# A first burst of eight query heads, output weights ahead of the fourth row tile, and the values transposed in two halves, in a fused attention and gated feed-forward kernel

## The chip, the cores and the metric

The kernel runs on one core of a Trainium2 chip. The core has five engines that work side by side, each on its own list of instructions: PE (TensorE, matrix products into the PSUM memory), ACT (ScalarE, functions of single elements), DVE (VectorE, element-wise work and reductions), POOL (GpSimd) and SP (SyncE, which here issues DMAs). An instruction that needs another engine's result waits for a semaphore, and all behind it on that engine waits too. The metric is the time of one execution on the device in microseconds, and of several runs the median.

## The reference

One layer: attention over a cached window of keys and values, times a gated feed-forward branch, plus the input. Cut to what is computed:

```
xn = layernorm(x)                                   # x: 2048 rows of 448
# attention: 16 query heads on 8 key/value heads of 256, the last 512 cached positions
q = (xn @ wq) in 16 heads
p = softmax(q @ k.T / 16)                           # no mask
s = concat(p @ v over the heads) @ wo
# gated feed-forward branch, 1792 wide
f = (gelu(xn @ w_gate) * (xn @ w_up)) @ w_down
out = x + s * silu(f)
```

All inputs and the output are bf16.

## The kernel before

The 2048 rows are four chunks (`NQC`) of 512 rows (`QC`), each of four tiles (`TPC`) of 128 rows. The kernel holds keys, values and weights in SBUF throughout. A recorder (`Rec`) collects the operations of each engine in the order in which the program calls them, and adds waits on semaphores where one operation needs what another writes, or writes what another still reads. So the order of the calls is the order on each engine. Three stages follow each other.

**Start (lines 301 to 441).** SP issues the loads in the order in which they are written: rows of tiles 0 and 1, the values of the last key/value head (`load_v7`), rows of tiles 2 and 3 (`load_x0`), the last head's rows of the output weights (`load_wo7`), then the feed-forward weights by slices. Two of the small weight loads go through ACT's queue. PE runs small matmuls on zeros (`warm`), then transposes the last head's values through the identity into one PSUM bank (`fold_tr`, L388), and ACT copies that bank to `vT` (`fold_copy`, L394). With `vT` and the loaded output weights PE makes `vw`, the product of the last head's values and their output weights (`fold`, L400, four products), so that the last head of each chunk goes straight from its probabilities to the output. Between these the first four tiles are normalised: statistics on DVE (L335, L336), standard deviation on ACT (L373), reciprocal and normalisation on DVE (L377, L339), transposes on PE (`ln_tr`, L357 and L359), and copies to `xnT` (`ln_copy`, L368 on DVE for tiles 2 and 3, L370 on ACT for tiles 0 and 1). On DVE the statistics of tiles 2 and 3 stand ahead of both their normalisations.

**Feed-forward (from `gate_up`).** For each chunk and each of 14 blocks `f` of the width, PE makes the gate and up products (L472), ACT applies gelu (L489) and DVE multiplies (L490). The row length of 448 is three and a half times 128, and so these products run as pairs of matmuls that use 64 rows of the array each, side by side (`two_blocks`). After each of the first three chunks PE makes the down products (`down`, L496). The last chunk's down products are kept for later: 4 tiles of 14 matmuls, which the table `fill` spreads over the first part of attention.

**Attention.** Head `i` counts from 0 to 63: sixteen heads for each of the four chunks. The queries of several heads are made at a time by a *burst* (`q_burst`, two_blocks again, 14 matmuls for each head), copied by ACT to the buffers `qT0` to `qT4` (L527), one for each pair of heads (`q_slot`). For each head and each row tile `t`, `scores(i, t)` makes one 128x512 product on PE (L552, two matmuls), the exponential with its row sum on ACT (L556), the reciprocal and scaling on DVE (L558, L559), and a DMA transpose of the probabilities `pr` to `pT`, issued by SP (`dmaT`, L252). The buffers `pr` are used in turn. Three heads behind, `values(i, e_)` multiplies `pT` by the values (L574), one half of the head's width at a time, and DVE copies the result to `oT`; it needs the transposes of all four tiles of its head. The output products (`outproj`, L604) follow later still, and DVE and POOL combine them with the feed-forward branch.

In this loop the order of the calls in one step is: `scores`; a share of `down` where `fill` has one; at even steps from the twelfth on, one `values`; at odd steps from head 7 on, a share of `outproj`; and the next burst of queries, if one is due. In the kernel before, the first burst is of four heads, ahead of the loop; the second, of four, comes after the step of head 3, tile 0; and then one of eight comes after tile 0 of heads 7, 15, 23 and so on.

Of the kernel before, what the change touches and what calls it, by code (L numbers as in the profile page):

```python
# [5 lines left out]
ACT = mybir.ActivationFunctionType  # L6
ALU = mybir.AluOpType
BF16 = mybir.dt.bfloat16
# [3 lines left out]
P = 128  # L12
# [132 lines left out]
def bass_recurrent_scan__sliding_block_cached__geglu_ffn__prompt_kernel(nc, A_x, A_k, A_v, A_wq, A_wo, B_x, B_wg, B_wu, B_wd, out):  # L145
    _, S, D = A_x.shape
    Hkv, Sk, Dh = A_k.shape[1], A_k.shape[2], A_k.shape[3]
    HD = A_wq.shape[1]
    Hq = HD // Dh
    W = min(4096, max(256, Sk // 4))  # L150
    F = B_wg.shape[1]
    QC, TPC, HP, KF = 512, 4, 64, 3
    NQC = S // QC
    NT = NQC * TPC
    NF, NJ, NE = F // P, W // P, Dh // P
# [6 lines left out]
    with es:  # L162
        off = [16512]

        def sb(name, shape, dt, at=None):
            n = 4 if dt == F32 else 2
            for x in shape[1:]:
                n *= x
            if at is None:
                at = off[0]  # L170
                off[0] += (n + 31) // 32 * 32
            return R.place(name, shape, dt, at), at + (n + 31) // 32 * 32

        ident, _ = sb("ident", [P, P], BF16)
# [11 lines left out]
        V, _ = sb("V", [P, NJ, Hkv, Dh], BF16)  # L186
# [20 lines left out]
        NPT, NQP = 4, 5  # L207
# [28 lines left out]
        def bank(b, n=512):  # L236
            return psum[:, b * 512:b * 512 + n]
# [5 lines left out]
        pe = lambda *a, **k: R.op("tensor", *a, **k)  # L243
        act = lambda *a, **k: R.op("scalar", *a, **k)
# [3 lines left out]
        def dma(eng, dst, src, w=(), r=(), after=(), lane=None):  # L248
            return R.op(eng, lambda e: e.dma_start(dst, src), r=r, w=w, dma=True, after=after, lane=lane)  # L249

        def dmaT(dst, src, w=(), r=(), after=(), lane=None):
# [9 lines left out]
             r=[("ident",)], w=[("ident",)])  # L261


        def load_x0(a, b):
            dma("sync", x4[:, a:b, :], x_view[:, 0, a:b, :], w=[("x4", t) for t in range(a, b)])
# [6 lines left out]
        def load_w(n, s):  # L272
            a, b = cuts[s] * P, cuts[s + 1] * P
            w, name, src, _ = w_gu[n]
            dma("sync", w[:, :, a:b], src[:, :, a:b], w=[(name, s)])

        def load_gu(s):
            load_w(0, s)
            load_w(1, s)
# [15 lines left out]
        def load_v7():  # L295
            dma("sync", V[:, :, Hkv - 1, :], v_view[:, :, Hkv - 1, :], w=[("V", "f")])

        def load_wo7():
            dma("sync", wo[:, NO - NE:NO, :], wo_v[:, NO - NE:NO, :], w=[("wo", "f")])
# [1 line left out]
        for t in range(2):  # L301
            load_x0(t, t + 1)
        load_v7()
        for t in range(2, TPC):
            load_x0(t, t + 1)
        load_wo7()
        load_gu(0)
        load_gu(1)
        load_gu6(5, NF, "sync")
# [71 lines left out]
        vT = actT[:, NF - 3:NF - 1, :]  # L381
        vT_keys = [("actT", NF - 3), ("actT", NF - 2)]

        def fold_tr():
            def run(e):
                for m in range(NE):
                    for j in range(NJ):
                        ins = e.transpose(bank(0).bitcast(BF16)[:, m * W + j * P:m * W + (j + 1) * P],  # L388
                                          V[:, j, Hkv - 1, m * P:(m + 1) * P], ident[:, :])
                return ins  # L390
            pe(run, r=[("V", "f"), ("ident",)], w=[("ps", 0)])

        def fold_copy():
            act(lambda e: e.activation(vT.rearrange("p m k -> p (m k)"), bank(0).bitcast(BF16), ACT.Copy),  # L394
                r=[("ps", 0)], w=vT_keys)

        def fold(j):
            def run(e):
# [12 lines left out]

        warm(32)
        fold_tr()
        for t in range(2):
            ln_stats(t)
# [48 lines left out]
        def two_blocks(ph, c, s, w, w6, keys, q0=0, q1=QC):  # L464


            def run(e):
                for k in range(KF + 1 - ph):
                    for lo in (0, HP):
                        m = (lo > 0) ^ ph  # L470
                        lhsT = w[m][lo:lo + HP, k, :] if k < KF else w6[lo:lo + HP, :]
                        ins = e.matmul(bank(s + m)[:, q0:q1], lhsT=lhsT, rhs=xnT[lo:lo + HP, c, k, q0:q1],  # L472
                                       start=ph == 0 and k == 0, stop=ph == 1 and k == KF - 1)
                return ins
            hard = [phase0[s]] if ph else []
            phase0[s] = pe(run, r=xn(c)[q0 // P:q1 // P] + keys, w=[("ps", s), ("ps", s + 1)], hard=hard)
# [30 lines left out]
        NI = NQC * Hq  # L507
        NG = NI // 4

        def q_slot(i):  # L510

            p = i // 2
            p = p if p < 3 else (p - 3) % NQP
            return qT[p], "qT%d" % p, i % 2

        def q_burst(i0, heads):

            c, h0 = divmod(i0, Hq)

            def part(n, ph):  # L520
                hp, e_ = divmod(n, 2)
                s, h = 2 * (n % 3 if heads == 8 else (0, 2, 1, 0)[n] if i0 else (n + 2) % 4), h0 + 2 * hp
                buf, name, _ = q_slot(i0 + 2 * hp)
                two_blocks(ph, c, s, [wq[:, :, h + m, e_ * P:(e_ + 1) * P] for m in range(2)],
                           wq6[:, h // 2, e_ * P:(e_ + 1) * P], wq_keys)
                if ph:
                    act(lambda e: e.activation(  # L527
                        buf[:, :, e_, :], psum[:, s * 512:(s + 2) * 512].rearrange("p (a q) -> p a q", a=2), ACT.Copy),
                        r=[("ps", s), ("ps", s + 1)], w=[(name, e_)])

            for n in range(heads + 1):
                if n < heads:
                    part(n, 0)
                if n:
                    part(n - 1, 1)
# [9 lines left out]
        def scores(i, t):  # L545
            g, n = (i % Hq) // 2, i * TPC + t
            b, s = 4 + n % 2, n % NPR
            buf, name, a = q_slot(i)

            def run(e):  # L550
                for k in range(NE):
                    ins = e.matmul(bank(b), lhsT=buf[:, a, k, t * P:(t + 1) * P], rhs=kT[:, g, k, :],  # L552
                                   start=k == 0, stop=k == NE - 1)
                return ins
            pe(run, r=[("kT", g), (name, 0), (name, 1)], w=[("ps", b)])
            act(lambda e: e.activation(pr[s][:, :], bank(b), ACT.Exp, scale=scale, accum_out=den[:, s:s + 1]),  # L556
                r=[("ps", b)], w=[("pr%d" % s,), ("den", s)])
            dve(lambda e: e.reciprocal(rden[:, s:s + 1], den[:, s:s + 1]), r=[("den", s)], w=[("rden", s)])  # L558
            dve(lambda e: e.tensor_scalar(pr[s][:, :], pr[s][:, :], rden[:, s:s + 1], None, op0=ALU.mult),  # L559
                r=[("pr%d" % s,), ("rden", s)], w=[("pr%d" % s,)])  # L560
            dst, key = p_slot(i)
            dmaT(dst[:, :, t * P:(t + 1) * P], pr[s][:, :], r=[("pr%d" % s,)], w=[(*key, t)], lane="p%d" % s)
# [22 lines left out]
        def n_pieces(G):  # L585
            return 3 * NE + NJ if folded(4 * G + 3) else 4 * NE
# [52 lines left out]
        def load_xr(c):  # L639
            dma("gpsimd", xr[:, :, :], x_view[:, c, :, :], w=[("xr", t) for t in range(TPC)])  # L640
# [11 lines left out]
        for c in range(NQC):  # L652
            lead = 6 if c == 0 else 2
            for f in range(NF + 1):
# [4 lines left out]
                t = (f - lead) // 2  # L659
# [13 lines left out]
                    load_piece()  # L673
        assert not pieces
        act(lambda e: e.activation(small[:, 2:3], small[:, 0:1], ACT.Exp), r=[("eps",)], w=[("warm",)])
        q_burst(0, 4)
        load_xr(0)

        fill = {}
        for d, slots in ((0, range(0, 4)), (1, range(4, 12)), (2, range(13, 17)), (3, range(17, 21))):  # L680
            for n, s in enumerate(slots):
                fill[s] = d, range(n * NF // len(slots), (n + 1) * NF // len(slots))
        pv = [(i, e_) for i in range(NI) if not folded(i) for e_ in range(NE)]
        outs = [(G, t) for G in range(NG) for t in range(TPC)]
        for i in range(NI):
            for t in range(TPC):
                scores(i, t)
                if 4 * i + t in fill:
                    down(NQC - 1, *fill[4 * i + t])

                early = i >= Hq and i % Hq == 2
                if t % 2 == 0 and early:
                    n = n_pieces(outs[1][0])
                    outproj(*outs[1], range(n * t // 4, n * (t + 2) // 4), b=6)
                elif t % 2 == 0 and 4 * i + t >= 12:
                    values(*pv.pop(0))
                if 7 <= i and t % 2 and not (i >= Hq and i % Hq == 6):
                    n = n_pieces(outs[0][0])
                    outproj(*outs[0], range(n * (t - 1) // 4, n * (t + 1) // 4))
                    if t == TPC - 1:  # L700
                        del outs[0:1 + early]
                if t == 0 and (i == 3 or i % 8 == 7) and i + 1 < NI:
                    q_burst(i + 1, 4 if i == 3 else 8)
            if i % Hq in (7, 9, 11, 13):
                silu(i // Hq * TPC + (i % Hq - 7) // 2)

# [40 lines left out]
```

## Time and profile before

| What | us |
|---|---|
| median of 3 runs | 558.26 (558.12 to 558.84) |
| the profiled execution | 558.57 |
| its span, first to last instruction | 556.8 |
| PE busy | 552.5 |
| ACT busy | 295.6 |
| DVE busy | 313.7 |
| first matmul of the feed-forward stage (L472) | at 10.39 |
| first matmul of the scores (L552) | at 133.56 |

The span is that of the program's own instructions; the rest of the execution's time lies around it. Times "at" are counted from the start of the span. The granted TensorE clock was 1.0 throughout. Matmuls are pipelined: the start of the next one is a better measure of what a matmul takes of PE than its own duration. In the timeline, a row gives the start, the length, the engine, the line of the kernel, the operation, what it writes and reads, and how many instructions were merged into it; in brackets stands how long the engine had been idle and what ended that. Rows of "SPq" and "ACTq" are the issuing of DMAs by these engines.

### The profile page before, as it was taken

How to read it: one execution, taken by the hardware profiler on the slowest of the kernel's cores; microseconds unless marked ns; L12 is line 12 of the kernel's file. 1: busy time of each engine (PE TensorE's matmuls, PEld its weight loads, DVE VectorE, ACT ScalarE, POOL GpSimd, SP SyncE). 2: the span in 40 equal slices, each digit the busy share in tenths (PEclk: the TensorE clock that was granted, in tenths of full speed). 3: DMA queues.
4: the chain of work that ended last, by engine and by line, in shares of the span. 5: the costliest groups of instructions: out<-in, count | busy, mean ns of one | idle time of the engine just before them, and what ended most of it. 6: DMA issues, size and time to landing. Idle time of an engine off the chain costs nothing.

```text
span 556.8 us, 9924 instructions
## 1 busy us (share of the span) xinstructions
PE 552.5 (99%) x3550; PEld 261.4 (47%) x3550; DVE 313.7 (56%) x822; ACT 295.6 (53%) x688; POOL 88.4 (16%) x125
## 2 busy tenths in 40 slices
PE   8999999999999999999999999999999999999997
PEld 6444444444444444444444444444444444444445
DVE  5535436043463678077728744772688077628775
ACT  5333324237655665555575556556665655575640
POOL 0131213200000121002301110131121002311134
DMA  8863534952544354245544552547345254635452
GB/s 233 292 140 70 132 86 95 233 146 54 98 86 77 58 98 93 58 85 94 129 75 96 101 95 39 96 95 143 66 96 101 42 86 97 130 79 105 95 96 52
DMA packets 165440, 57.65 MB, mean 104 GB/s; under 512 B 155648, under 2 KB 162304, under 8 KB 165392
## 3 DMA queue, kind: packets, MB, share of 16 engines
q1 hardware_dynamic: 162048, 44.64, 41.5%
q0 software_dynamic: 3040, 12.16, 8.0%
q8 instruction: 28, 0.46, 0.4%
q10 hardware_dynamic: 304, 0.22, 0.1%
q14 instruction: 20, 0.16, 0.1%
HBM read 17.92 MB, written 1.84 MB: 35 GB/s over the span
## 4 chain that ended last, share of the span: by engine, by line
PE 98%; DMA 1%; ACT 0%; SPq 0%; DVE 0%; issue 0%
PE ps L472 33%; PE ps L552 20%; PE ps L574 19%; PE ps L604 18%; PE ps L496 8%; DMA V<-in_A_v_cache_dram 1%; PE ps L400 0%; PE ps L388 0%; ACT actT L394 0%; SPq L249 0%; ACT xnT L370 0%; PE ps L357 0%; ACT std L373 0%; DVE tmp L615 0%; DVE xr L617 0%
## 5 line engine op out<-in xcount | busy, mean ns | idle before, releaser
L556 ACT ACTIVATE pr<-ps 128x512 bf16<-128x512 f32 x256 | 152.5, 597 | 120.4 <-PE ps L552 119.1
L552 PE MATMUL ps<-kT,qT 128*128 128x512 bf16 x512 | 150.9, 380 | 0.0
L558 DVE RECIPROCAL rden<-den 128x1 f32<-128x1 f32 x256 | 41.4, 162 | 154.2 <-ACT pr L556 139.6
L574 PE MATMUL ps<-pT,V 128*128 128x512 bf16 x480 | 123.1, 379 | 0.0
L559 DVE TENSOR_SCALAR pr<-pr,rden 128x512 bf16<-128x512 bf16 x256 | 106.0, 414 | 9.0
L604 PE MATMUL ps<-wo,oT 128*128 128x448 bf16 (+1 forms) x498 | 111.0, 346 | 0.0
L472 PE MATMUL ps<-xnT,wq 64*128 64x512 bf16 x896 | 98.3, 377 | 0.0
L527 ACT ACTIVATE qT<-ps 128x1024 bf16<-128x1024 f32 x64 | 64.5, 1022 | 43.4 <-PE ps L472 43.1
L472 PE MATMUL ps<-xnT,wu 64*128 64x512 bf16 x336 | 82.4, 377 | 0.0
L472 PE MATMUL ps<-xnT,wg 64*128 64x512 bf16 x336 | 82.0, 377 | 0.0
L581 DVE CAST oT<-ps 128x512 bf16<-128x512 f32 x118 | 80.5, 683 | 0.7 <-PE ps L574 0.6
L490 DVE TENSOR_TENSOR actT<-ps,hb 128x512 bf16<-128x512 f32 x56 | 38.5, 692 | 65.9 <-ACT hb L489 61.7
L552 PEld LDWEIGHTS ps<-kT,qT 128*128 128x128 bf16 x512 | 49.2, 98 | 55.4 <-issue 4.0
L574 PEld LDWEIGHTS ps<-pT,V 128*128 128x128 bf16 x480 | 47.0, 98 | 56.3
L604 PEld LDWEIGHTS ps<-wo,oT 128*128 128x128 bf16 x498 | 48.4, 98 | 48.6 <-DVE acc L627 1.0
L472 PEld LDWEIGHTS ps<-xnT,wq 64*128 64x128 bf16 x896 | 43.1, 94 | 54.5 <-DVE rden L558 1.7
L489 ACT ACTIVATE hb<-ps 128x512 bf16<-128x512 f32 x56 | 33.1, 593 | 38.8 <-PE ps L472 38.6
L556 ACT ACTIVATION_READ_ACCUMULATOR pr<-ps 128x1 f32 x256 | 50.2, 196 | 0.0
L496 PE MATMUL ps<-wd,actT 128*128 128x448 bf16 x224 | 46.2, 353 | 0.0
L472 PEld LDWEIGHTS ps<-xnT,wg 64*128 64x128 bf16 x336 | 31.3, 94 | 20.5 <-issue 1.1
L472 PEld LDWEIGHTS ps<-xnT,wu 64*128 64x128 bf16 x336 | 31.3, 94 | 19.9
L646 POOL TENSOR_SCALAR tmp<-tmp 128x448 f32<-128x448 f32 x16 | 9.0, 563 | 197.9 <-ACT tmp L645 197.9
(60 smaller groups left out, 264.0 us busy)
## 6 DMA issues: line engine op xcount, KB each, us to landing
pT<-pr SPq DMA_TRANSPOSE x240, 2.5
wq<-in_A_wq_dram POOLq DMA_DIRECT2D x14, 256.0 KB, 3.6
wo<-in_A_wo_dram POOLq DMA_DIRECT2D x3, 896.0 KB, 9.0
V<-in_A_v_cache_dram POOLq DMA_DIRECT2D x4, 448.0 KB, 6.5
xr<-in_A_x_dram POOLq DMA_DIRECT2D x4, 448.0 KB, 4.2
wd<-in_B_w_down_dram SPq DMA_DIRECT2D x1, 1568.0 KB, 15.1
x<-in_A_x_dram SPq DMA_DIRECT2D x3, 448.0 KB, 9.3
out_dram<-xr POOLq DMA_DIRECT2D x3, 448.0 KB, 3.7
```

The lines of the kernel that those rows point to most:

```text
L472: ins = e.matmul(bank(s + m)[:, q0:q1], lhsT=lhsT, rhs=xnT[lo:lo + HP, c, k, q0:q1], start=ph == 0 and k == 0, stop=ph == 1 and k == KF - 1)
L489: act(lambda e: e.activation(hb[:, h, :], bank(s), ACT.Gelu_apprx_tanh), r=[("ps", s)], w=[("hb", h)])
L490: dve(lambda e: e.tensor_tensor(actT[:, f, :], bank(s + 1), hb[:, h, :], ALU.mult), r=[("ps", s + 1), ("hb", h)], w=[("actT", f)])
L496: pe(lambda e, f=f: e.matmul(bank(b, D), lhsT=actT[:, f, t * P:(t + 1) * P], rhs=wd[:, f, :], start=f == 0, stop=f == NF - 1), r=[("actT", ...
L527: act(lambda e: e.activation(buf[:, :, e_, :], psum[:, s * 512:(s + 2) * 512].rearrange("p (a q) -> p a q", a=2), ACT.Copy), r=[("ps", s), ...
L552: ins = e.matmul(bank(b), lhsT=buf[:, a, k, t * P:(t + 1) * P], rhs=kT[:, g, k, :], start=k == 0, stop=k == NE - 1)
L556: act(lambda e: e.activation(pr[s][:, :], bank(b), ACT.Exp, scale=scale, accum_out=den[:, s:s + 1]), r=[("ps", b)], w=[("pr%d" % s,), ("de ...
L558: dve(lambda e: e.reciprocal(rden[:, s:s + 1], den[:, s:s + 1]), r=[("den", s)], w=[("rden", s)])
L559: dve(lambda e: e.tensor_scalar(pr[s][:, :], pr[s][:, :], rden[:, s:s + 1], None, op0=ALU.mult), r=[("pr%d" % s,), ("rden", s)], w=[("pr%d ...
L574: ins = e.matmul(bank(b), lhsT=V[:, j, g, e_ * P:(e_ + 1) * P], rhs=src[:, j, :], start=j == 0, stop=j == NJ - 1)
L581: dve(lambda e: e.tensor_copy(dst, bank(b)), r=[("ps", b)], w=[key])
L604: ins = e.matmul(bank(b, D)[:, lo:hi], lhsT=lhsT, rhs=rhs, start=idx == 0, stop=idx == n8 - 1)
```

## The change

There are three edits, and a table that goes with the first.

- The first burst of queries makes eight heads instead of four, and the burst of four after head 3 is gone. Pair `p` of heads goes to buffer `p % 5` throughout. The last chunk's down products are spread evenly: five steps for each of the four tiles, steps 0 to 19, where before it was steps 0 to 3, 4 to 11, 13 to 16 and 17 to 20.
- SP issues the load of the output weights for the last head ahead of the rows of the fourth tile, not behind them.
- The transposes of the last head's values go to two PSUM banks, four to each, and ACT copies each bank by an instruction of its own.

```diff
-        for t in range(2, TPC):
-            load_x0(t, t + 1)
+        load_x0(2, 3)
         load_wo7()
+        load_x0(3, 4)
...
         def fold_tr():
-            def run(e):
-                for m in range(NE):
-                    for j in range(NJ):
-                        ins = e.transpose(bank(0).bitcast(BF16)[:, m * W + j * P:m * W + (j + 1) * P],
-                                          V[:, j, Hkv - 1, m * P:(m + 1) * P], ident[:, :])
+            def run(e, m):
+                for j in range(NJ):
+                    ins = e.transpose(bank(m).bitcast(BF16)[:, j * P:(j + 1) * P], V[:, j, Hkv - 1, m * P:(m + 1) * P], ident[:, :])
                 return ins
-            pe(run, r=[("V", "f"), ("ident",)], w=[("ps", 0)])
+            for m in range(NE):
+                pe(lambda e, m=m: run(e, m), r=[("V", "f"), ("ident",)], w=[("ps", m)])
 
         def fold_copy():
-            act(lambda e: e.activation(vT.rearrange("p m k -> p (m k)"), bank(0).bitcast(BF16), ACT.Copy),
-                r=[("ps", 0)], w=vT_keys)
+            for m in range(NE):
+                act(lambda e, m=m: e.activation(vT[:, m, :], bank(m).bitcast(BF16)[:, 0:W], ACT.Copy),
+                    r=[("ps", m)], w=[vT_keys[m]])
...
-            p = i // 2
-            p = p if p < 3 else (p - 3) % NQP
+            p = i // 2 % NQP
             return qT[p], "qT%d" % p, i % 2
...
-                s, h = 2 * (n % 3 if heads == 8 else (0, 2, 1, 0)[n] if i0 else (n + 2) % 4), h0 + 2 * hp
+                s, h = 2 * (n % 3 if i0 else (n + 2) % 4), h0 + 2 * hp
...
-        q_burst(0, 4)
+        q_burst(0, 8)
...
-        for d, slots in ((0, range(0, 4)), (1, range(4, 12)), (2, range(13, 17)), (3, range(17, 21))):
+        for d, slots in ((0, range(0, 5)), (1, range(5, 10)), (2, range(10, 15)), (3, range(15, 20))):
...
-                if t == 0 and (i == 3 or i % 8 == 7) and i + 1 < NI:
-                    q_burst(i + 1, 4 if i == 3 else 8)
+                if t == 0 and i % 8 == 7 and i + 1 < NI:
+                    q_burst(i + 1, 8)
```

## The prediction

> **What bounds the kernel now.** I read the page first: the busy times, then the chain that ended last.
>
> ```profile
> PE 552.5 (99%) x3550; PEld 261.4 (47%) x3550; DVE 313.7 (56%) x822; ACT 295.6 (53%) x688; POOL 88.4 (16%) x125
> q8 instruction: 28, 0.46, 0.4%
> PE 98%; DMA 1%; ACT 0%; SPq 0%; DVE 0%; issue 0%
> ```
>
> The chain is PE from 10.4 us to the end, and in the list of waits PE waits for nothing after 7.8 us. So the time is the start (until the first matmul of L472) plus PE's own work plus whatever stalls a change brings in. An edit that moves work off other engines gains nothing; one that makes PE wait costs its wait in full. The timeline of the first 22 us shows the start:
>
> ```profile
> 3.13 0.43 SPq L249 DMA_DIRECT2D wo<-in_A_wo_dram  x1
> 5.81 1.02 ACT L394 ACTIVATE actT<-ps 128x1024 bf16<-128x1024 bf16 x1 [1.09 <-PE ps L388]
> 6.57 0.63 DVE L335 BATCH_NORM_STATS2 stats<-x 128x6 f32<-128x448 bf16 x1 [0.44 <-DMA x<-in_A_x_dram]
> 6.93 0.62 PE L347 MATMUL ps<-actT 128*128 128x128 bf16 x8
> 7.78 1.29 PE L400 MATMUL ps<-wo,actT 128*128 128x448 bf16 x6 [0.23 <-ACT std L373]
> 8.00 0.40 DVE L339 TENSOR_SCALAR xn<-x,mv,rstd 128x448 bf16<-128x448 bf16 x1
> 8.91 0.33 PE L357 MATMUL ps<-ident,xn 128*128 128x128 bf16 x3
> 9.35 0.34 PE L357 MATMUL ps<-ident,xn 128*128 128x128 bf16 x3
> 9.46 0.88 DVE L368 COPY xnT<-ps 128x512 bf16<-128x512 bf16 x2 [1.06 <-PE ps L359]
> 10.39 0.39 PE L472 MATMUL ps<-xnT,wg 64*128 64x512 bf16 x1
> ```
>
> PE waits before L400 at 7.78. The row names a standard deviation on ACT, but the wo load lands 4.5 us after its issue (7.64, by the list of DMA issues) and the copy of the values is done at 6.83: the wait is wo's, and costs about 0.34 us (the gap in starts, 0.45, less the 0.11 that one small matmul takes). Tile 3's rows land at 6.54 and start the statistics at 6.57. Then I read the stretch where attention begins, engine by engine:
>
> ```profile
> 133.02 1.94 ACT L527 ACTIVATE qT<-ps 128x1024 bf16<-128x1024 f32 x2 [0.49 <-PE ps L472]
> 133.56 0.60 PE L552 MATMUL ps<-kT,qT 128*128 128x512 bf16 x2
> 136.19 17.25 SPq L252 DMA_TRANSPOSE pT<-pr  x12
> 144.48 1.03 PE L574 MATMUL ps<-pT,V 128*128 128x512 bf16 x4
> 145.44 6.22 PE L472 MATMUL ps<-xnT,wq 64*128 64x512 bf16 x56
> 151.59 0.61 PE L552 MATMUL ps<-kT,qT 128*128 128x512 bf16 x2
> ```
>
> I call one scores(i, t) slot 4i+t. SP issues one transpose of pr for each slot. From 136.19 to 144.01 it issued six, 1.30 us each, while PE and ACT passed a slot in some 0.8 to 1.1 us: here SP is slower than PE. It catches up while PE spends 6.15 us in the second burst at 145.44. The latest single issue and the landing times:
>
> ```profile
> 151.02 2.42 SPq L252 DMA_TRANSPOSE pT<-pr  x1
> DMA to landing us min/median/max: 2.4/2.5/5.7
> 169.96 1.03 PE L574 MATMUL ps<-pT,V 128*128 128x512 bf16 x4
> 170.91 12.26 PE L472 MATMUL ps<-xnT,wq 64*128 64x512 bf16 x112
> ```
>
> At 169.96, in slot 28, PE takes values(4, 0), which needs the transpose of slot 19. That landed at 165.31, 4.64 us early.
>
> **The change part by part.** *One burst less.* PE's matmuls are the same in number; 56 of the burst at 145.44 move ahead of slot 0. What goes is one change from 128-row to 64-row matmuls and back. The four matmuls of L574 from 144.48 to the burst took 0.96 us, while four at 169.09 took 0.87 to the next start: 0.09 for going in. The burst took 6.15 where 28 pairs at 0.216 make 6.05: 0.10 for coming out. Gain 0.19 us. The Trainium skill ("TensorEngine Tiling (Array Packing)", Key Properties) says that a change of tiling mode drains TensorE; the rows agree in direction, and it gives no price.
>
> *SP loses its pause.* This is the step that decides. In both kernels the first transpose can be issued 2.63 us after the first score (136.19 - 133.56), since exp(0) waits for the last two qT copies and both first bursts end alike. The transpose of slot 19 is then issued 19 x 1.308 = 24.85 us later (1.308: median gap between issues that wait for no data) and lands 2.47 later: 29.95 after the first score if nothing disturbs it. In the same stretch of before two things did. The twelfth issue came 0.48 late (at 151.02, the eleventh at 149.23 + 1.31); such a pause of 0.30 recurs at three later places, 64 issues apart. And it took 2.42 in place of some 1.2. Single long issues of 1.92, 2.23, 2.35, 2.03 and 2.41 us stand at 192.27, 216.53, 258.99, 300.04 and 325.76, each within 0.8 us of one of the 28 packets of the instruction queue (151.71, 192.23, 217.18, 259.75, 300.70, 325.57); over all such places in full trains the excess is 0.5 to 1.4, mean 0.93. There is one such packet for some 253 of PE's 7,100 instructions, so it follows PE's count: the one at 151.71 comes 18.15 us after the first score, and with 6.15 us of the matmuls counted before the first score it will come at about 12.0, inside SP's train; its neighbours fall before the first transpose and at some 34.6.
>
> PE, for its part, needs from the first score to values(4, 0) 169.96 - 133.56 = 36.40 us now. Without the burst that is 36.40 - 6.25 = 30.15 (6.25: from 145.34, where the next matmul would have started, to 151.59). All 56 matmuls of L496 still lie before it. The landing: undisturbed 29.95; with the smallest disturbances (0.30 + 0.55) 30.80; as measured in this stretch of before 31.75, less 0.14 that SP waited there for slot 19's own row, 31.61; with the largest (0.48 + 1.42) 31.85. I take 31.61, the nearest row. PE starts 0.05 after a landing (V landed at 4.70, L388 started at 4.75). So PE stalls 31.66 - 30.15 = 1.5 us; bounds 0 and 1.75. The wait stands in PE's queue ahead of the burst of 112 matmuls and all after it, and ACT's eight copies of that burst wait with it. During that burst (12.2 us) SP works off the rest, as now, so the stall is paid once. Earlier deadlines hold: values(3, 0) in slot 24 is due at 30.15 - 3.45 = 26.70, and slot 15's transpose lands 5.23 before slot 19's, at 26.4.
>
> The Trainium skill ("DMA: Bandwidth & Descriptors", Issuing engines are not separate DMA queues) calls the sequencer's time to initiate a DMA usually small beside the DMA. Here it is 1.26 of 2.5 us. By the page SP would never be late, and the sum would lack the 1.5.
>
> *The other orders in the middle.* Fill slots shift 56 matmuls of L496 to slots 0 to 19: PE then takes 0.81 or 1.0 us a slot in slots 0 to 11 where ACT needs 0.81 (0.60 and 0.21), so ACT keeps up. If it did not, PE would lose at most 0.2 a slot. Pair p of qT goes to buffer p mod 5; every buffer was last read some heads before. Cost 0, covered by PE's work.
>
> *wo ahead of tile 3's rows.* Only the two SP issues swap (0.43 each); no other queue is passed. The rings are first in, first out, so wo lands earlier, and tile 3's rows last of the two: about when wo landed, 7.64 instead of 6.54. PE's fold can start at 7.44 (after eight warm matmuls), a gain of at most 0.34. But tile 3 is late next: from its landing to the end of norm(3) is 8.40 - 6.54 = 1.86, 0.05 to L357, 0.55 from there to the second L368 copy, 0.48 to L472: 2.94 in all. On DVE norm(2) stands behind its statistics as well. Landing at 7.64 gives L472 at 10.58: 0.19 late. Bounds: the rows land by 7.1 and all 0.34 is gained; or on the slowest DMA engines they take as long again behind wo as they did behind tile 2 (6.54 - 5.03 = 1.5), landing at 8.3: L472 at 11.24, 0.86 late. I take 0.19, since bytes ahead in the ring are the same.
>
> *Two halves.* One ACT copy of 1.02 becomes two of 0.59 (row L370), the first begun after four transposes: vT ready near 6.4, not 6.83. Eight warm matmuls until 7.44 cover it. Without that cover it would be worth 0.4; here 0.
>
> Sum: -0.19 + 1.51 + 0.19 = +1.5 us. The span goes from 556.8 to 558.3, the profiled execution from 558.57 (1.77 outside the span) to 560.1. The median of the runs before is 0.31 below that execution: 558.26 + 1.5 = 559.7.
>
> **The rivals.** *SP is in time* (the other side). Place: values(4, 0), slot 28. It decides at 30.10 us after the first score: if slot 19's transpose lands before, the stall is 0 and what is left is -0.19 + 0.19: 558.3. For it: undisturbed SP makes 29.95. Against: both disturbances occurred in this very train.
>
> *Fetching instructions costs SP nothing.* Then only the 0.48 remains: landing 30.43, stall 0.33, time 558.26 + 0.33 = 558.6. The Trainium skill ("Runtime: NRT & Kernel Launch", Instruction fetch mechanics) says that the sequencer fetches the next block by its own DMA and that crossing a block is mostly hidden. That holds for PE here; SP's 2.42 beside the packet speaks against it.
>
> *Tile 3 is the worse half.* The stall as forecast and the start 0.86 late: 558.26 - 0.19 + 1.51 + 0.86 = 560.4. For it: two DMA engines brought these rows 0.9 us after the other 14.
>
> *The reorder does what it says*: the fold gains 0.34 and the rows are in time: 558.26 - 0.19 + 1.51 - 0.34 = 559.2. Against: 112 KB now stand behind 224 KB, and DVE already idled 0.44 for them.
>
> **How the numbers follow.** About 0.2% (1.1 us) can be told from no change. Forecast 0.60, with its own range 558.9 to 560.3 (three quarters of it above 559.4); SP in time 0.09; free fetch 0.09; tile 3 worse 0.13; full gain at the start 0.05; a gain over 0.2% by something not seen here 0.04. Slower: 0.45 + 0.13 = 0.58; faster 0.04; the rest, 0.38, within 0.2%. The range reaches to the two small cases below and tile 3 above: 558.2 to 560.7.
>
> **What will show it.** In the changed profile: PE waiting for a pT transpose at the values of slot 28, just before the first later burst, and nowhere else; SP issuing without a break from the first transpose to past slot 28; nine groups of L472 bursts become eight; L400 starting near 7.4, the last statistics later than 6.57, and the first L472 near 10.6. I am wrong if PE shows no wait there, if the long issue falls outside SP's train, or if the first L472 comes before 10.3.

## The result, and the profile after

The changed kernel takes 559.56 us (median of 21 runs, 559.16 to 560.12) against 558.30 us (21 runs, 557.85 to 559.05): 1.26 us or 0.23% slower, ratio 1.0020, 95% interval 1.0014 to 1.0027. The forecast was 559.7 us in a range of 558.2 to 560.7.

The two profiled executions differ by less than the medians: spans of 556.8 and 557.4 us, times of 558.57 (0.27 above its median) and 559.22 (0.34 below). The difference lies in the start, as will be seen. Of the page after:

```profile
PE 549.2 (99%) x3518; PEld 262.2 (47%) x3550; DVE 313.5 (56%) x822; ACT 296.5 (53%) x689; POOL 88.5 (16%) x125
PE 97%; issue 1%; DMA 1%; DVE 0%; SPq 0%; ACT 0%; ACTq 0%
```

PE is still nearly the whole chain. The count has to be read first: 3,518 matmuls for 3,550 weight loads, so 32 matmul records are missing. Each leaves a gap of one matmul (0.216 us), which the chain books as "issue"; these are no waits. From PE's list of waits, after, the two rows that count:

```profile
PE ps L573 <- DVE rden L557: 1.1, 1, 1.1
PE ps L357 <- DVE xn L339: 0.4, 1, 0.4
```

The first is new, one wait at the values (L573, which was L574). Its named releaser, a reciprocal on DVE, is only the event nearest in time. The timeline of that stretch, after (start, length, engine, line, operation):

```profile
165.24 7.77 SPq L252 DMA_TRANSPOSE pT<-pr  x6
168.44 1.03 PE L551 MATMUL ps<-kT,qT 128*128 128x512 bf16 x4
170.57 0.56 PEld L573 LDWEIGHTS ps<-pT,V 128*128 128x128 bf16 x4 [1.60 <-issue]
170.60 1.02 PE L573 MATMUL ps<-pT,V 128*128 128x512 bf16 x4 [1.13 <-DVE rden L557]
171.56 0.61 PE L472 MATMUL ps<-xnT,wq 64*128 64x512 bf16 x4
```

The scores of slots 27 and 28 start at 168.44 and take four times 0.216, so PE could have gone on at 169.30. It goes on at 170.60: 1.30 us late. The transpose of slot 19 is this row:

```profile
167.85 1.22 SPq L252 DMA_TRANSPOSE pT<-pr  x1
```

It landed 2.50 us after its issue, at 170.36, where in before it was 4.64 us early. SP issues without a break, six in 7.77 us.

At the start of attention, after:

```profile
139.28 0.38 PE L551 MATMUL ps<-kT,qT 128*128 128x512 bf16 x1 [0.16 <-issue]
140.30 0.73 PE L496 MATMUL ps<-wd,actT 128*128 128x448 bf16 x3
140.34 0.60 ACT L555 ACTIVATE pr<-ps 128x512 bf16<-128x512 f32 x1
141.09 0.61 PE L551 MATMUL ps<-kT,qT 128*128 128x512 bf16 x2
```

The row at 139.28 holds one matmul where two belong: the first is not recorded and started at 139.06. Three matmuls of 0.189 from 140.30 end their turn at 140.87, but the scores of slot 2 start at 141.09. They need the bank that the exponential of slot 0 reads, and this began only at 140.34, behind ACT's last copy of queries. That is a second wait, of 0.21 us, which I had not foreseen.

The start, after:

```profile
2.67 0.43 SPq L249 DMA_DIRECT2D wo<-in_A_wo_dram  x1
3.14 0.47 SPq L249 DMA_DIRECT2D x<-in_A_x_dram  x1
5.01 1.08 ACT L394 ACTIVATE actT<-ps 128x512 bf16<-128x512 bf16 x2 [0.31 <-PE ps L387]
6.56 1.30 PE L400 MATMUL ps<-wo,actT 128*128 128x448 bf16 x6
6.86 0.63 DVE L335 BATCH_NORM_STATS2 stats<-x 128x6 f32<-128x448 bf16 x1 [0.76 <-DMA x<-in_A_x_dram]
8.24 0.34 PE L357 MATMUL ps<-ident,xn 128*128 128x128 bf16 x3 [0.38 <-DVE xn L339]
9.84 0.37 PE L472 MATMUL ps<-xnT,wg 64*128 64x512 bf16 x1
```

Tile 3's rows now come last (DVE waits 0.76 for them), and PE waits for the normalised rows at 8.24, no more for the weights at L400. L472 starts at 9.84 instead of 10.39, so this execution won 0.55 us there.

The books of PE from the first L472 to the start of the last matmul: 543.24 us before, 544.44 after, +1.20. Its items: one pair of mode changes less, -0.19; a wait of 0.10 right after the second burst of before (between L552 and L496 at 152.13), which is gone with that burst and whose cause is open; +0.21 at slot 2; +1.30 at slot 28. Together +1.22.

### The profile page after: what moved, and what is told of

It is laid out like the page before. It is cut to its first block, busy times and chain, and to the rows that moved or that the text cites. A ratio compares the mean times of both kernels' runs of the same rounds, so it can differ in the third digit from the quotient of the medians.

```text
span 557.4 us, 9893 instructions
## 1 busy us (share of the span) xinstructions
PE 549.2 (99%) x3518; PEld 262.2 (47%) x3550; DVE 313.5 (56%) x822; ACT 296.5 (53%) x689; POOL 88.5 (16%) x125
## 4 chain that ended last, share of the span: by engine, by line
PE 97%; issue 1%; DMA 1%; DVE 0%; SPq 0%; ACT 0%; ACTq 0%
PE ps L472 33%; PE ps L551 19%; PE ps L573 19%; PE ps L603 18%; PE ps L496 7%; DMA x<-in_A_x_dram 1%; SPq L249 0%; ACT pr L555 0%; PE ps L357 0%; DVE stats L335 0%; PE ps L400 0%; DVE xn L339 0%; DVE tmp L614 0%; DVE xr L616 0%; PE ps L359 0%
## 5 line engine op out<-in xcount | busy, mean ns | idle before, releaser
L551 PE MATMUL ps<-kT,qT 128*128 128x512 bf16 x489 | 145.7, 379 | 2.1 <-issue 1.3
L573 PE MATMUL ps<-pT,V 128*128 128x512 bf16 x471 | 121.7, 379 | 1.6 <-DVE rden L557 1.1
L472 PE MATMUL ps<-xnT,wq 64*128 64x512 bf16 x896 | 98.1, 376 | 0.0
L472 PE MATMUL ps<-xnT,wu 64*128 64x512 bf16 x336 | 82.5, 376 | 0.0
L472 PE MATMUL ps<-xnT,wg 64*128 64x512 bf16 x336 | 81.8, 376 | 0.1
L573 PEld LDWEIGHTS ps<-pT,V 128*128 128x128 bf16 x480 | 46.9, 98 | 57.6 <-issue 1.6
L472 PEld LDWEIGHTS ps<-xnT,wq 64*128 64x128 bf16 x896 | 43.0, 94 | 54.4 <-DVE rden L557 1.3
L496 PE MATMUL ps<-wd,actT 128*128 128x448 bf16 x224 | 46.2, 353 | 0.0
L472 PEld LDWEIGHTS ps<-xnT,wg 64*128 64x128 bf16 x336 | 31.3, 94 | 20.0 <-issue 1.3
L472 PEld LDWEIGHTS ps<-xnT,wu 64*128 64x128 bf16 x336 | 31.2, 94 | 19.2
```

Of the source, the lines that this page charges most:

```text
L496: pe(lambda e, f=f: e.matmul(bank(b, D), lhsT=actT[:, f, t * P:(t + 1) * P], rhs=wd[:, f, :], start=f == 0, stop=f == NF - 1), r=[("actT", ...
L573: ins = e.matmul(bank(b), lhsT=V[:, j, g, e_ * P:(e_ + 1) * P], rhs=src[:, j, :], start=j == 0, stop=j == NJ - 1)
```

## The experiments

All times are medians beside runs of the kernel before on the same chip; "a to b" behind a ratio is the 95% interval.

**e1: the first edit alone.** The kernel before with the burst of eight, the table of down products and `p = i // 2 % NQP`; the start as before.

> The kernel before with the first edit alone (first burst of eight heads, the table of down products, the buffers of qT). SP theory: PE loses 1.3 us at the values of slot 28 and gains 0.19 from the burst that is gone, so +1.1 us over before, and the trace shows PE idle there until slot 19's transpose has landed. Rival (the 1.26 us come from the start's new load order): -0.2 us, and the wait at slot 28 is not what makes the time.

559.74 against 558.4 us, ratio 1.0022 (1.0013 to 1.003): +1.3 us. The timeline of e1, PE alone:

```profile
168.76 1.03 PE L551 MATMUL ps<-kT,qT 128*128 128x512 bf16 x4
171.04 1.02 PE L573 MATMUL ps<-pT,V 128*128 128x512 bf16 x4 [1.25 <-DVE rden L557]
```

From 168.76 + 0.86 = 169.62 to 171.04 PE waits 1.42. So the first edit alone has the whole loss, and the wait with it.

**e2: the second edit alone; e3: the third alone; e10: both.** Diff of e2 (e3 is the change of `fold_tr` and `fold_copy` as shown above):

```diff
-        for t in range(2, TPC):
-            load_x0(t, t + 1)
+        load_x0(2, 3)
         load_wo7()
+        load_x0(3, 4)
```

> The kernel before with the second edit alone (output weights ahead of the fourth tile's rows). Theory: the later of the two loads decides in both orders, 2.75 us ahead of L472 when it is the weights and 2.94 us when it is the rows: +0.2 us (0 to 0.3), and L472 starts 2.94 after the rows land. Rival (the fold waited for the weights, and the rows have time): -0.3 us. Rival (the changed profile's early L472, 9.84, comes of the order): -0.5 us.

> The kernel before with the third edit alone (values transposed into two banks, two ACT copies). Theory: hidden behind the eight warm matmuls and the weights' load: within 0.1 us of before, L394 done some 0.4 us earlier, L400 still at the landing of the weights. Rival (the copy is on the path): -0.4 us.

> The kernel before with both start edits and not the first. By e2 and e3 (each -0.1, with intervals of some 0.5 either way): -0.1 (-0.4 to +0.2). My prediction's sum for them: +0.2. Rival (the changed profile's L472 at 9.84, 0.55 early, comes of these edits): -0.5.

e2: 558.3 against 558.4, ratio 0.9998 (0.9989 to 1.0006). e3: 558.27 against 558.4, 0.9998 (0.9989 to 1.0006). e10: 558.29 against 558.47, 0.9996 (0.9987 to 1.0005). None can be told from before; neither my +0.2 nor a gain of 0.3 is resolved. A gain of 0.5 us isn't excluded either: in us, e2's interval is -0.6 to +0.3 and e10's -0.7 to +0.3. But the trace of e10 shows that these edits need not bring the early L472 of the changed profile:

```profile
6.98 1.29 PE L400 MATMUL ps<-wo,actT 128*128 128x448 bf16 x6
7.48 0.63 DVE L335 BATCH_NORM_STATS2 stats<-x 128x6 f32<-128x448 bf16 x1 [1.36 <-DMA x<-in_A_x_dram]
8.86 0.34 PE L357 MATMUL ps<-ident,xn 128*128 128x128 bf16 x3 [0.58 <-DVE xn L339]
10.40 0.39 PE L472 MATMUL ps<-xnT,wg 64*128 64x512 bf16 x1
```

With the same two edits the fold starts early (6.98, before at 7.78), the rows land at 7.45, and L472 starts at 10.40, as late as in before. Over all profiles of this study L472 starts between 9.52 and 10.39 with the old order (six profiles, mean 10.04) and between 9.59 and 10.40 with the new (eight, mean 9.98). In the old order the weights land last, at 6.77 to 7.64 (mean 7.20); in the new the rows, at 6.40 to 7.45 (mean 6.92). The two means of L472 are 0.06 apart, while single profiles of one order differ by up to 0.9: no gain or loss is shown here.

**e4: the burst of slot 28 ahead of that slot's values**, in the changed kernel; **e7: the same with the old start.**

```diff
                 early = i >= Hq and i % Hq == 2
+                if t == 0 and i == 7:
+                    q_burst(i + 1, 8)
...
-                if t == 0 and i % 8 == 7 and i + 1 < NI:
+                if t == 0 and i % 8 == 7 and i != 7 and i + 1 < NI:
```

> The changed kernel with the burst of slot 28 put ahead of the values of slot 28 in PE's order. SP theory: the 12.2 us of the burst cover the transpose, PE waits nowhere, and the 1.3 us come back: 1.3 below the changed kernel, 0.0 (-0.2 to +0.2) against before. Rival (the loss is elsewhere): stays 1.2 above before.

> The kernel before with the first edit and the burst of slot 28 put ahead of the values of that slot, the start unchanged. SP theory: no wait, one pair of mode changes less: -0.2 against before (-0.3 to 0). Rival: a wait elsewhere takes its place, +0.5 or more.

e4: 558.71 against 558.4, ratio 1.0006 (0.9995 to 1.0017): by the medians, most of the 1.26 came back and 0.3 did not, where I had expected 0.0 (-0.2 to +0.2). e7: 558.68 against 558.3, 1.0003 (0.9995 to 1.0012), where I had expected -0.2: a miss. The timeline of e7 shows why, and e4's trace has the same gap:

```profile
168.26 1.03 PE L551 MATMUL ps<-kT,qT 128*128 128x512 bf16 x4
169.67 1.69 PE L472 MATMUL ps<-xnT,wq 64*128 64x512 bf16 x14 [0.39 <-DVE oT L580]
```

From 169.12 (168.26 + 0.86) plus 0.10 for the mode change to 169.67 the burst waits 0.45 for DVE's copy to oT: the values of slot 26 wrote bank 1, and the burst begins in banks 0 and 1. The wait for SP's transpose is gone, and a smaller one for DVE stands in its place.

**e8 and e9: the same with that burst beginning in banks 2 and 3**, with the old and the new start.

```diff
-                s, h = 2 * (n % 3 if i0 else (n + 2) % 4), h0 + 2 * hp
+                s, h = 2 * ((1, 0, 2)[n % 3] if i0 == 8 else n % 3 if i0 else (n + 2) % 4), h0 + 2 * hp
```

> e7 with the burst of slot 28 beginning in PSUM banks 2 and 3 instead of 0 and 1 (e7's trace has PE waiting 0.45 us there for DVE's copy of bank 1, which the values of slot 26 wrote). Theory: that wait goes, PE waits nowhere, and one pair of mode changes less is left: -0.2 against before (-0.5 to 0), 0.45 below e7. Rival (the next thing in line, ACT's exponentials of banks 4 and 5, waits instead): no better than e7.

> The changed kernel with the burst of slot 28 ahead of the values and beginning in banks 2 and 3. Theory: 1.4 below the changed kernel, -0.2 against before, as e8; the two starts do not differ by what can be measured. Rival (the new start is worth the 0.2 to 0.5 us that its profile shows): 0.3 below e8.

e8: 558.11 against 558.47, ratio 0.9994 (0.9985 to 1.0003). e9: 558.27 against 558.47, 0.9996 (0.9987 to 1.0005). Their medians lie 1.45 and 1.29 us below that of the changed kernel; neither can be told from before, nor one from the other. In e8's timeline no wait is left at slot 28:

```profile
168.62 1.03 PE L551 MATMUL ps<-kT,qT 128*128 128x512 bf16 x4
169.57 12.26 PE L472 MATMUL ps<-xnT,wq 64*128 64x512 bf16 x112
181.77 1.04 PE L573 MATMUL ps<-pT,V 128*128 128x512 bf16 x4
```

168.62 + 0.86 + 0.10 is 169.58: the burst starts when PE is free, and the values after it find their transpose 11 us old (it landed at 170.75).

**e5 and e6: one more transpose on SP**, in the changed kernel and in the kernel before.

```diff
+            if n == 5:
+                dmaT(pT[:, 3, :, 0:P], pr[s][:, :], r=[("pr%d" % s,)], w=[("pT", 3, 0)])
```

> The changed kernel with one more DMA transpose on SP, behind that of slot 5, into a part of pT that is written again before it is read. SP theory: SP's train is one issue (1.31 us) longer, so the transpose of slot 19 lands 1.31 later and PE's wait at slot 28 grows from 1.3 to 2.6: +1.3 over the changed kernel, +2.5 over before. Rival (SP is not what PE waits for): 0 over the changed kernel.

> The kernel before with the same additional transpose. SP theory: its margins are 1.92 us at slot 12 and 4.64 us at slot 28, both over 1.31, so nothing: within 0.1 of before. Rival (any additional issue costs its time): +1.3.

e5: 561.27 against 558.3, ratio 1.0047 (1.0034 to 1.0061), so 1.9 to 3.4 us over before: +1.7 over the changed kernel by the medians, where 1.3 was expected. e6: 558.19 against 558.3, 0.9996 (0.9987 to 1.0005): nothing. Timeline of e5:

```profile
164.75 1.03 PE L551 MATMUL ps<-kT,qT 128*128 128x512 bf16 x4
166.50 1.02 PE L575 MATMUL ps<-pT,V 128*128 128x512 bf16 x4 [0.72 <-DVE rden L557]
169.09 1.03 PE L551 MATMUL ps<-kT,qT 128*128 128x512 bf16 x4
171.76 1.02 PE L575 MATMUL ps<-pT,V 128*128 128x512 bf16 x4 [1.65 <-DVE pr L558]
```

PE now waits at slot 24 too (0.89 from 165.61) and at slot 28 (1.81 from 169.95): 2.70 together, 1.40 more than the 1.30 of the changed kernel. One issue on SP (1.31) costs the changed kernel about its whole length and the kernel before nothing: SP is what PE waits for.

**e11: PE's instruction packets shifted**, in the changed kernel, by small matmuls in the third chunk's down products; they add to bank columns that nobody reads.

```diff
+                if c == 2 and 1 <= f <= 11:
+                    pe(lambda e, f=f: e.matmul(bank(b)[:, D:D + 32], lhsT=actT[:, f, t * P:(t + 1) * P], rhs=wd[:, f, 0:32],
+                                               start=False, stop=False), r=[("actT", f), ("wd",)], w=[("ps", b)])
```

> The changed kernel with 44 matmuls of 32 columns added to the third chunk's down products, into columns of the bank that nobody reads. Each costs some 0.03 to 0.1 us, 1.5 to 4.5 us in all, all of it ahead of attention. With their weight loads they are 88 more instructions on PE, so the two instruction packets now at 10.1 and 33.3 us after the first transpose's issue come some 9 us earlier, at about 1 and 24, both inside SP's train ahead of slot 19. Theory (such a packet delays a transpose): two long issues instead of one, slot 19's transpose lands about 0.9 (0.5 to 1.4) later after the first issue than the 28.7 of the changed kernel, and PE's wait at slot 28 grows from 1.3 by as much. Rival (chance, or the place in SP's own list): one long issue, the ninth, and a wait of 1.3.

A single run, 560.46 us, so its time decides nothing; its trace does. The first of two packets came as planned, 1.0 us after the first issue. The second came 29.9 after that issue, not 24, and so behind slot 19's issue. Why the two stand 28.9 apart and not 23 is open. So the doubling wasn't tried after all; the shift was. The long issue in the changed kernel, and then in e11:

```profile
152.11 2.16 SPq L252 DMA_TRANSPOSE pT<-pr  x1
```

```profile
144.23 1.96 SPq L252 DMA_TRANSPOSE pT<-pr  x1
```

In the changed kernel it is the ninth issue (10.4 us after the first; the packet starts at 10.07). In e11 it is the second, with the packet at 1.0 us after the first issue, and the ninth has its ordinary length. The long issue goes with the packet, not with a place in SP's list. The total hardly moves, since there is still one long issue ahead of slot 19: its transpose lands 28.61 us after the first issue (28.67 in the changed kernel) and PE waits 1.24.

**e12: e9 with more down products in the first slots.**

```diff
-((0, range(0, 5)), (1, range(5, 10)), (2, range(10, 15)), (3, range(15, 20)))
+((0, range(0, 4)), (1, range(4, 9)), (2, range(9, 14)), (3, range(14, 20)))
```

> e9 with the first tile's down products back in steps 0 to 3 (three and four a step, not two and three) and the others in 4 to 8, 9 to 13 and 14 to 19. e9's trace has PE 0.21 us late at the scores of slot 2: they wait for the exponential of slot 0, which ACT can begin only after the last qT copy. Theory: with three down products in slot 0 and four in slot 1 that wait goes, and from the first L472 to the last matmul PE takes 543.2 us, where e9 takes 543.4 and before 543.5. The median is 0.2 below e9, 0.3 to 0.5 below before, hardly more than its interval. Rival (the gap at 140.84 is a matmul that was not recorded): 543.4 again.

558.14 against 558.64, ratio 0.9993 (0.9984 to 1.0002). The wait at slot 2 is gone. PE in e9 and then in e12:

```profile
140.06 0.73 PE L496 MATMUL ps<-wd,actT 128*128 128x448 bf16 x3
140.84 0.60 PE L551 MATMUL ps<-kT,qT 128*128 128x512 bf16 x2
```

```profile
141.00 0.92 PE L496 MATMUL ps<-wd,actT 128*128 128x448 bf16 x4
141.75 0.59 PE L551 MATMUL ps<-kT,qT 128*128 128x512 bf16 x2
```

In e9, three times 0.189 after 140.06 is 140.63, and the scores start 0.21 later. In e12, four times 0.189 after 141.00 is 141.76, and the scores follow at once. All 3,550 matmuls are recorded in both, so e9's gap is real. From the first L472 to the start of the last matmul PE takes 543.15 us in e9, 542.94 in e12 and 543.24 in before. So in these traces e12 takes 0.30 us less on PE than the kernel before, which is the 0.19 and the 0.10 of the burst that is gone. By the medians it is 0.5 below before, but its interval still holds no change.

## Why the prediction was right

**The step that decides held.** The place (values of slot 28), the cause (SP's train of transposes without the pause of the second burst) and the consequence (one wait, paid once, ahead of the next burst) are as forecast, shown by e1 (the edit alone), e5 and e6 (the cost lengthened) and e8 and e9 (the wait taken away by order alone).

| Term | predicted us | measured us |
|---|---|---|
| one burst less | -0.19 | -0.30 on PE in e12, of which 0.10 is the wait after that burst |
| the table of down products | 0 | +0.21 |
| wait at slot 28 | +1.51 | +1.30 (e1: +1.42) |
| load order at the start | +0.19 | not resolved; e2 -0.1 (-0.6 to +0.3) |
| two halves | 0 | not resolved; e3 -0.1 (-0.6 to +0.3) |

The wait: PE was free 30.24 us after the first score (predicted 30.15), the transpose landed at 31.30 (predicted 31.61), and PE started 0.24 behind the landing (predicted 0.05, from a load at the start). Both disturbances of SP that I took from the stretch in before came again: the pause ahead of the twelfth issue (0.48) and one long issue beside an instruction packet, at 12.7 after the first score (predicted 12.0), of 2.16 instead of 2.42.

That the time came within 0.2 us of the forecast is in part luck. The wait at slot 28 was 0.21 smaller than forecast, the 0.10 behind the old burst was not in my sum, and the +0.19 of the start didn't show; a wait of 0.21 at slot 2, which I had put at nothing, made up for a part of this.

**The step that failed is "ACT keeps up"** in the table of down products. I compared PE's 0.81 to 1.0 us a slot with ACT's 0.81 and left out that ACT begins its first exponential 1.3 us after the first score in both kernels (134.85 before, 140.34 after), behind the last two copies of queries. Steps 0 and 1 held seven down products before and five after; 0.38 us of cover went with them. My bound for that case, 0.2 a slot, fits the 0.21, and it was paid at one slot. e12, which gives the two steps seven again, takes the wait away.

**The start** was mis-sized too, and whether it costs or gains anything stays open. 2.94 us from the landing of the rows to L472 holds where the rows decide (9.84 - 6.84 = 3.00 after; 10.40 - 7.45 = 2.95 in e10). But the landing of 7.64 was that of one execution, the latest of six in the old order, and I put the new order's landing at that value. That execution lay 0.3 above the median, which was the hint. So two of my signs failed here: L400 came at 6.56 and not near 7.4, and the first L472 at 9.84, before 10.3, which I had named as a sign of being wrong. It speaks against this term, not against the wait at slot 28.

**The rivals.** SP in time and free instruction fetch are refuted by the landing at 31.30 (they needed 30.10 and 30.43) and by e11's long issue. Tile 3 as the worse half and the full gain at the start are not seen in the medians. The chance of 0.58 for a loss over 0.2% met a loss of 0.23% whose interval begins at 0.14%.

## What to carry to other kernels

On a kernel whose matrix engine never waits, removing an overhead on that engine also removes time in which a slower queue catches up. Follow every producer whose rate is below the consumer's from its first item to the first deadline, with its disturbances, and see which pause lets it catch up; here 0.19 us of mode changes paid for 1.3 us of waiting. If the pause can stand just ahead of the deadline instead of behind it (e8, e9), the gain can be kept, but look at who last used the buffers that move up with it (e7).

## What the runs showed of the hardware

- A matmul that waited for a DMA transpose started 0.24 us after the landing: landing at 170.36 in the changed kernel, two semaphore instructions on PE at 170.38 and 170.50, weight load at 170.57. At the start of the kernel, behind a single load, it was 0.05.
- A DMA transpose from SBUF to SBUF took SP 1.2 to 1.3 us to issue, and 17 issues in before's attention and feed-forward stages and 16 in the changed kernel's took over 1.6 us (1.72 to 2.64 and 1.76 to 2.87). Of these 16 and 14 began within 0.8 us of a packet of the instruction queue; not every packet had a long issue beside it. With 88 instructions more on PE (e11) the first long one of the train moved from the ninth issue to the second. The pause of some 0.4 to 0.5 us, in contrast, stays with SP's own list: with one issue more (e5) it still stood ahead of the twelfth issue.
- The first 10 us vary by up to 0.9 us between executions (L472 at 9.52 to 10.40). L472 followed the later of the two loads, weights or rows, by 2.75 to 3.00 us in 12 of the 14 profiles. The first small matmuls differ too: the eight transposes of the values took 1.03 us in before's profile and 0.62 in the changed one. For comparison, the 21 runs of the kernel before lie within 1.20 us.
- A small matmul of 32 columns between larger ones cost 0.025 us (e11: 1.12 us for 44, from the first L472 to the first score).
